# Loading half of the spectral filters behind the first bounce, and fewer feed-forward weights ahead of D

## The chip, the cores and the metric

The kernel runs on one core of a Trainium2 chip. The metric is device time in microseconds (us). Executions of one kernel mostly agree within 0.3%; the kernel before took 892.1 to 895.99 us in the runs that the prediction was made from.

Engines are called as in the profile: PE is TensorE (PEld its weight loads), DVE is VectorE, ACT is ScalarE, POOL is GpSimd, SP is SyncE, which here only issues DMAs. Every trace time is in us from the start of the span.

## The reference

Two layers, one behind the other. The first is a spectral filter over the sequence, the second a gated feed-forward block:

```
X = rfft(x, axis=1)              # x: 8 x 3008 x 256
y = irfft(X * (filt_r + 1j*filt_i), n=3008)
gate = maximum(y @ w_gate, 0)    # 256 x 1536
val  = y @ w_val                 # 256 x 1536
out  = (gate * val) @ w_out      # 1536 x 256
```

## The kernel before

The transform of length 3008 = 94 x 32 is done by matmuls in two stages. Stage A transforms over 94 and writes A to memory (`Abuf`); reading it back as `at` regroups it. I call this write and read the first bounce. Stage B, for six groups i: a forward matmul (`psX`), products with the filters (`tt` with the real part `Ftr`, `uu` with the imaginary part `Fti`), and an inverse matmul (`psD`) whose result D goes to memory (`Dbuf`). D comes back as `dC` (second bounce); stage C (`psY`) and the feed-forward matmuls V, G (`psV`, `psG`) and O (`psO`) follow. The first batch's B has nothing beside it; the later ones hide amid the feed-forward.

The filters lie in two copies along the partitions: GpSimd's DMA loads one, casting to bf16, and a copy (`place_filter`) makes the other. The code below is shortened; `...` stands where lines or arguments are left out.

```python
def load_filters():                      # eight loads, upper and lower groups together
    for src, dst in FILT:                # FILT = ((filt_r, Ftr), (filt_i, Fti))
        for a in range(2):
            r, k1, n = a * 64, 1 + 24 * a, NG - 2 * a
            nc.gpsimd.dma_start(dst[r:r + 31:2, 0:n, :], ...)       # rows that lie together
            yield
            nc.gpsimd.dma_start(dst[r + 1:r + 32:2, 0:n, :], ...)   # rows in reversed order

def place_filter(fi, a, half, copy):
    ...                                  # dst is Ftr or Fti, gs the half's groups, r = 64 * a
    copy(dst[r + 32:r + 64, gs, :], dst[r:r + 32, gs, :])

POOL_U = ((0, 1), (1, 0), (1, 1), (2, 0), (2, 1), (3, 1), (4, 0))   # products on GpSimd

def product(b, i, e, k, pool=False):
    ...
    if pool:
        nc.scalar.copy(xs, psX)                         # a copy for GpSimd to read
        nc.gpsimd.tensor_tensor(p, xs, filt, op=ALU.mult)
    else:
        nc.vector.tensor_tensor(p, psX, filt, op=ALU.mult)

def first_b(amid):
    ...
    for i in range(6):
        fwd(0, i)
        if i > 1:
            inv(0, i - 2, cuts=cuts)
        for e in range(2):
            product(0, i, e, 0)
            product(0, i, e, 1, pool=(i, e) in POOL_U)
        amid(i)                 # warming matmuls, then stage A of the next batch
    inv(0, 4, cuts=cuts); amid(6); inv(0, 5, cuts=cuts)
```

In the order of the program (cut):

```python
    next(filters)               # the first filter load, ahead of x
    ...                         # loads of x; the other seven wait for x's first half
    # stage A, load_at, then on DVE and ACT: all eight placements, place_nyq
    for i in range(14):
        warm(2)                 # idle matmuls that keep TensorE's clock up
    load_x(1, nc.sync, ((0, 0, 2 * q), (0, 2 * q, 4 * q), (1, 0, 4 * q)))   # the next batch
    ...
    hold_gpsimd(ats[0][0:32, NG - 1, 0:8])     # GpSimd waits for the first bounce
    load_vg(0, DFF // 2)                       # half of V's and G's weights
    first_b(amid)
    ...
    load_d(0, 0, 2)
    nc.gpsimd.dma_start(last, Dbuf[0][...])    # GpSimd waits for D's last write
    for c in range(2, 4):
        load_vg(c * DFF // 4, (c + 1) * DFF // 4)
```

## Time and profile before

| what (trace of the kernel before) | value |
|---|---|
| span of the profiled run | 892.0 us |
| first forward matmul of B (`psX`), end of the first bounce | 34.34 |
| third inverse (the one after the fifth forward): first 2 of its 16 matmuls | 43.02 |
| third inverse: the other 14, which wait for ScalarE's copies | 43.38 |
| last write of D issued | 51.03 |
| first stage C matmul (`psY`) | 57.35 |
| first O matmul (`psO`) | 72.59 |

TensorE is busy 98% of the span, and behind the first O matmul nothing else sets the pace. So whatever moves the first O matmul moves the end. The chain of waits shows which stage ends on what, the DMA use by queue shows who holds the 16 engines, and the timeline shows each engine's line. The prediction below shows those lines. One name there is off by one: what it calls "the one after the fourth forward" is the inverse behind the fifth, the third of six.

### The profile page before, as it was taken

To read this page: it belongs to the slowest core of one execution; us is meant where nothing else is said; L and a number is where in the kernel's file an instruction comes from. 1 tells how busy PE (TensorE), PEld (TensorE's weight loads), DVE (VectorE), ACT (ScalarE), POOL (GpSimd) and SP (SyncE) were. 2 spreads that over 40 slices of the span, in tenths; PEclk is the share of its full clock that TensorE was granted. 3 is DMA by queue.
4 is the path that set the end of the run, shared out by engine and by line. 5 is a ranking of instruction groups with operands and counts; after the bars stand their busy time and mean duration, and the time that the engine had idled before them with its cause. 6 is when DMAs were issued, how large, how long until landed. Compare 5 with 4: busy or idle time off the path is not lost.

```text
span 892.0 us, 19155 instructions
## 1 busy us (share of the span) xinstructions
PE 875.7 (98%) x7208; PEld 506.8 (57%) x7208; DVE 567.1 (64%) x871; ACT 504.2 (57%) x893; POOL 364.4 (41%) x361
## 2 busy tenths in 40 slices
PE   7899999999999999999999999999999999999997
PEld 2335655566556665566655565556655566666665
DVE  2736776577665766667766677657776577655553
ACT  4675555555655566556555556555655555555553
POOL 4350697038651476316671176802867000000001
PEclk9999999999999999999999999999999999999999
DMA  9997448534456336453376334662446512331111
GB/s 244 305 235 141 143 138 166 119 102 130 120 142 133 116 97 155 130 125 97 96 174 146 86 102 109 175 139 78 116 141 148 121 31 81 76 79 36 37 32 53
DMA packets 114099, 109.18 MB, mean 122 GB/s; under 512 B 20359, under 2 KB 98599, under 8 KB 113366
## 3 DMA queue, kind: packets, MB, share of 16 engines
q1 hardware_dynamic: 90294, 80.10, 34.7%
q0 software_dynamic: 22992, 26.41, 12.3%
q8 instruction: 57, 0.93, 0.5%
q10 hardware_dynamic: 720, 1.45, 0.4%
q14 instruction: 36, 0.29, 0.1%
HBM read 61.93 MB, written 49.81 MB: 125 GB/s over the span
## 4 chain that ended last, share of the span: by engine, by line
PE 93%; DMA 3%; ACT 1%; POOL 1%; issue 1%; DVE 0%; SPq 0%; ACTq 0%; POOLq 0%
PE psV L467 28%; PE psG L467 27%; PE psO L486 27%; PE psF L323 3%; PE psY L451 2%; PE psD L394 2%; PE psX L364 2%; PE psA L276 2%; DMA dC<-Dbuf 1%; DMA Abuf<-asb 1%; DMA at<-Abuf 1%; DMA XF<-in_x_dram 1%; ACT dsb L401 0%; DMA Dbuf<-dsb 0%; SPq L176 0%
## 5 line engine op out<-in xcount | busy, mean ns | idle before, releaser
L472 DVE SCALAR_TENSOR_TENSOR prod<-psG,vsb 128x512 bf16<-128x512 f32 x564 | 389.2, 690 | 263.6 <-ACT vsb L470 258.1
L470 ACT CAST vsb<-psV 128x512 bf16<-128x512 f32 x564 | 331.8, 589 | 263.0 <-PE psV L467 170.9
L467 PE MATMUL psV<-yT,WvT 128*128 128x512 bf16 x1128 | 336.6, 380 | 0.7 <-ACT asb L330 0.4
L486 PE MATMUL psO<-WoT,prod 128*128 128x256 bf16 x2256 | 336.5, 273 | 0.0
L467 PE MATMUL psG<-yT,WgT 128*128 128x512 bf16 x1128 | 335.4, 379 | 0.7 <-ACT dsb L401 0.3
L486 PEld LDWEIGHTS <-prod 128*128 128x128 bf16 x2256 | 220.2, 98 | 143.8
L467 PEld LDWEIGHTS <-WgT 128*128 128x128 bf16 x1128 | 109.9, 97 | 135.9 <-issue 2.5
L467 PEld LDWEIGHTS <-WvT 128*128 128x128 bf16 x1128 | 98.4, 98 | 41.9 <-issue 30.4
L258 POOL CAST scr<-prod 128x8 f32<-128x8 bf16 x24 | 4.5, 189 | 258.3 <-DVE prod L472 258.3
L509 POOL DMA_DIRECT2D out_dram<-osb x5 | 2.6, 536 | 195.9 <-ACT osb L499 195.9
L499 ACT COPY osb<-psO 128x512 f32<-128x512 f32 x92 | 53.9, 586 | 27.6 <-PE psO L486 26.1
L380 DVE TENSOR_TENSOR tt<-psX,Ftr 128x512 bf16<-128x512 f32 x96 | 65.1, 682 | 5.9 <-PE psX L364 5.9
L309 POOL TENSOR_TENSOR fold<-XP 128x1024 f32<-128x1024 f32 x24 | 56.5, 2355 | 20.5 <-PE psF L323 19.2
L380 DVE TENSOR_TENSOR uu<-psX,Fti 128x512 bf16<-128x512 f32 x89 | 60.6, 681 | 0.0
L401 ACT CAST dsb<-psD 128x512 bf16<-128x512 f32 x96 | 51.5, 589 | 12.1 <-PE psD L394 11.8
L296 POOL DMA_DIRECT2D XP<-in_x_dram x96 | 56.7, 596 | 3.2 <-PE psG L467 1.6
L310 POOL TENSOR_TENSOR XP<-XP 128x1024 f32<-128x1024 f32 x24 | 56.4, 2349 | 1.9
L330 ACT CAST asb<-psF 128x512 bf16<-128x512 f32 x48 | 25.8, 589 | 30.5 <-PE psF L323 30.5
L330 DVE CAST asb<-psF 128x512 bf16<-128x512 f32 x48 | 30.9, 686 | 18.6 <-PE psF L323 18.6
L456 ACT CAST yT<-psY 128x512 bf16<-128x512 f32 x47 | 27.5, 586 | 23.8 <-PE psY L451 23.6
L451 PE MATMUL psY<-M,dC 96*128 96x94 bf16 (+18 forms) x604 | 37.7, 199 | 1.4 <-DMA dC<-Dbuf 1.2
L458 DVE CAST yT<-psY 128x512 bf16<-128x512 f32 x47 | 32.0, 681 | 9.8 <-PE psY L451 9.8
(72 smaller groups left out, 493.5 us busy)
## 6 DMA issues: line engine op xcount, KB each, us to landing
at<-Abuf SPq DMA_DIRECT2D x32, 384.0 KB
dC<-Dbuf SPq DMA_DIRECT2D x64, 192.0 KB
XP<-in_x_dram POOLq DMA_DIRECT2D x48, 256.0 KB, 6.1
Dbuf<-dsb SPq DMA_DIRECT2D x23, 512.0 KB
XP<-in_x_dram POOLq DMA_DIRECT2D x96, 96.0 KB, 2.7
Abuf<-asb SPq DMA_DIRECT2D x96, 96.0 KB
out_dram<-osb SPq DMA_DIRECT2D x69, 94.0 KB
XF<-in_x_dram SPq DMA_DIRECT2D x15, 256.0 KB
```

Of the source, the lines that this page charges most:

```text
L296: nc.gpsimd.dma_start(xp[r:r + 24, 0:4:2, :], _ap(x, (b * N1 * N2 + o) * D, [[N2 * D, 24], [47 * N2 * D, 2], [1, 512]]))
L309: tt(t, xp[:, 0:2], xp[:, 2:4], op=ALU.add)
L310: tt(xp[:, 2:4], xp[:, 0:2], xp[:, 2:4], op=ALU.subtract)
L330: copy(asf[:, :, q, :], banks[q])
L380: nc.vector.tensor_tensor(p, psX, filt, op=ALU.mult)
L401: nc.scalar.copy(dsb[:, a, o:o + 2, :], psD[a])
L451: nc.tensor.matmul(psY[:, o:o + w], dCs[b, n2 // 8][:, n2 % 8, h * 128:(h + 1) * 128], M1[:, n1:n1 + w], start=True, stop=True)
L467: nc.tensor.matmul(pt[:, :W], w[:, h, ft * 128:(ft + 1) * 128], yt[:, h, :], start=(h == 0), stop=(h == 1))
L470: nc.scalar.copy(vsb, psV[:, :W])
L472: nc.vector.scalar_tensor_tensor(prod, in0=psG[:, :W], scalar=0.0, in1=vsb, op0=ALU.max, op1=ALU.mult)
L486: nc.tensor.matmul(psO[:, t % 2], prods[ft][:, t * 128:(t + 1) * 128], WoT[:, ft, :], start=(ft == 0), stop=(ft == NFT - 1))
L499: copy(osb[:, t0 % 2:t % 2 + 1], psO[:, t0 % 2:t % 2 + 1])
```

## The change

The filters' loads are cut into a lower and an upper half of the groups. The lower half stays where it was. The upper half is issued once the first bounce has landed, and placed on VectorE amid the first B, ahead of the products of group 3, the first that need it. GpSimd, now busy with issues, gives its products in groups 0 and 1 to VectorE and takes others. To leave the queue room, only a quarter of V's and G's weights goes ahead of D. Six warming matmuls go. The intent is to free the DMA engines for the first bounce.

```diff
-    def load_filters():
+    def load_filters(half):
+        g0 = H * half
         for src, dst in FILT:
             for a in range(2):
-                r, k1, n = a * 64, 1 + 24 * a, NG - 2 * a
+                r, k1, n = a * 64, 1 + 24 * a, H - 2 * a * half
 ... (both loads on groups g0 to g0 + n)
-    POOL_U = ((0, 1), (1, 0), (1, 1), (2, 0), (2, 1), (3, 1), (4, 0))
+    POOL_U = ((2, 0), (2, 1), (3, 0), (3, 1), (4, 0), (4, 1))
 ... (in first_b, behind fwd(0, i))
+            if i == 3:
+                for fi in range(2):
+                    for a in range(2):
+                        place_filter(fi, a, 1, nc.vector.tensor_copy)
+                place_nyq()
 ... (ahead of the first B: four placements of the lower half, all on VectorE)
-    for i in range(14):
+    for i in range(11):
         warm(2)
 ...
-    load_vg(0, DFF // 2)
+    for _ in load_filters(1):
+        pass
+    load_vg(0, DFF // 4)
 ...
-    for c in range(2, 4):
+    for c in range(1, 4):
         load_vg(c * DFF // 4, (c + 1) * DFF // 4)
```

More of the change, by code (lines that the diff above doesn't have):

```diff
@@ L213 @@
     nyq = []
-    def load_filters():
+    def load_filters(half):
+        g0 = H * half
         for src, dst in FILT:
             for a in range(2):
-                r, k1, n = a * 64, 1 + 24 * a, NG - 2 * a
-                nc.gpsimd.dma_start(dst[r:r + 31:2, 0:n, :],
-                                    _ap(src, k1 * D, [[N1 * D, 16], [1, n * D]]))
+                r, k1, n = a * 64, 1 + 24 * a, H - 2 * a * half
+                nc.gpsimd.dma_start(dst[r:r + 31:2, g0:g0 + n, :],
+                                    _ap(src, (k1 + g0) * D, [[N1 * D, 16], [1, n * D]]))
                 yield
-                nc.gpsimd.dma_start(dst[r + 1:r + 32:2, 0:n, :],
-                                    _ap(src, (N1 - k1) * D, [[N1 * D, 16], [-D, n], [1, D]]))
+                nc.gpsimd.dma_start(dst[r + 1:r + 32:2, g0:g0 + n, :],
+                                    _ap(src, (N1 - k1 - g0) * D, [[N1 * D, 16], [-D, n], [1, D]]))
     def load_own_filters():
@@ L525 @@
     nc.scalar.dma_start(tabs, nc.inline_tensor(tab_h, name="dft_tab").ap())
-    filters = load_filters()
+    filters = load_filters(0)
     next(filters)
@@ L550 @@
     warm(6)
-    place_filter(0, 1, 0, nc.scalar.copy)
     for i in range(3):
         make_back_u(i)
-    for a, half in ((0, 0), (0, 1), (1, 1)):
-        place_filter(0, a, half, nc.vector.tensor_copy)
     place_own()
-    for a, half, copy in ((1, 0, nc.scalar.copy), (0, 0, nc.vector.tensor_copy),
-                          (0, 1, nc.vector.tensor_copy), (1, 1, nc.vector.tensor_copy)):
-        place_filter(1, a, half, copy)
-    place_nyq()
-    for i in range(14):
+    for fi in range(2):
+        for a in range(2):
+            place_filter(fi, a, 0, nc.vector.tensor_copy)
+    for i in range(11):
         warm(2)
```

## The prediction

> **What bounds the kernel now.** I read the page first, then the chain that ended last up to the first block, then DMA use by queue in short windows, then the timeline there.
>
> ```profile
> PE 875.7 (98%) x7208; PEld 506.8 (57%) x7208; DVE 567.1 (64%) x871; ACT 504.2 (57%) x893; POOL 364.4 (41%) x361
> ```
>
> TensorE is busy 98% of 892 us. From about 60 us on, the chain is an unbroken run of V, G and O matmuls, so no later stage can give or take much. The change touches the first 75 us only, and the end moves by what moves the matmuls of the first block. The chain there (start, us, what):
>
> ```profile
> 12.82 10.53 PE psA L276 x24
> 23.37 0.59 ACT asb L279
> 23.98 5.43 DMA Abuf<-asb
> 29.47 4.78 DMA at<-Abuf
> 34.34 0.46 PE psX L364 x8
> ...
> 51.03 2.41 DMA Dbuf<-dsb
> 53.45 0.33 SPq L427
> 53.83 3.39 DMA dC<-Dbuf
> 57.35 0.62 PE psY L451 x12
> ```
>
> Stage A ends at 23.4 on TensorE; then comes the first bounce (A to memory and back), 10.4 us to the first psX at 34.34; then the first B, 16.7 us from there to the last write of D at 51.03; then the second bounce to 57.35. TensorE has 0.5 us of idle time in front of psY, so D's date sets the start of the first block. DMA by queue (packets, MB, share of 16 engines) in 18 to 22 us, then 22 to 26:
>
> ```profile
> q0 software_dynamic: 632, 0.61, 100.7%
> q1 hardware_dynamic: 56, 0.23, 15.0%
> ...
> q0 software_dynamic: 635, 0.47, 75.8%
> q1 hardware_dynamic: 180, 0.62, 41.1%
> ```
>
> q0 carries the filters, q1 the bounce. The filters hold the engines while A's writes want them: the packet records show A's second chunk written only at 21.1 to 23, though its last copy ended at 17.1, and the fourth, issued at 23.98, landing at 29.4. That wait is the change's target.
>
> **What the skill says.** The page DMA: Bandwidth & Descriptors, section Issuing engines are not separate DMA queues, says that queues of all issuers interleave on the same 16 engines; the same page, section SWDGE vs HWDGE vs iDMA, that a load which casts must be issued from GpSimd. The trace agrees: the filters (float to bf16) are on q0, and above q0 and q1 share one capacity. Its section Anatomy of one DMA gives some 2 us of fixed cost per GpSimd load. Here the issues of 34.84 had their first packet at 38.99, 4.1 us, and the first held filter load of 13.34 at 16.9, 3.5 us; with the engines free (54.58 to 56.85) it was 2.3 us. I use these.
>
> **Part 1: half of the filters leaves the bounce.** q0's shares in 14 to 30 us are 30.2, 100.7, 75.8 and 9.8% of four 4 us windows, 8.7 us of all engines. Half is 4.4 us. The backlog then ends near 23 us, just before A's last chunk is issued, which that issue at 23.98 bounds. Its landing should take about 3 us instead of 5.43. The return read, 3072 packets of 512 B, runs at 192 packets in 0.305 us once undisturbed, so 4.9 us; it began at 26.7 and had a straggling tail to 34.0. I expect it from 26.0 to 31.2, with a small tail: psX at about 31.9, so **2.4 us earlier** (1.5 to 3). VectorE's four placements (0.95 us each, row below) and 22 warming matmuls fit: they end near 30 and 31.
>
> **Part 2: the upper half is needed in the first B.** It is issued after the bounce, so its price is a new wait. The rows:
>
> ```profile
> L238 DVE COPY Ftr<-Ftr x3: 944/949/952, 25.8 to 27.6; 32x3072 bf16<-32x3072 bf16 x3
> L378 POOL TENSOR_TENSOR uu<-xs,Fti x7: 1143/1154/1156, 37.4 to 45.6; 128x512 bf16<-128x512 f32 x7
> ```
>
> GpSimd issues eight loads. In the timeline seven took 13.34 to 17.13, 0.54 us each, so 4.3 us. Starting 0.45 us after psX (31.9) they run 32.35 to 36.7, then V's and G's quarter (2 x 0.73) to 38.1. The first packet follows 3.5 to 4 us after the first issue: about 36.1. On q1 the next batch's x is flowing then. In the kernel before, its share was 95.9% in 35 to 40 us, against the weights' 5.3%, and the weights moved only afterwards:
>
> ```profile
> q1 hardware_dynamic: 228, 1.79, 95.9%
> q0 software_dynamic: 27, 0.04, 5.3%
> ...
> q0 software_dynamic: 436, 0.64, 72.9%
> q1 hardware_dynamic: 203, 0.55, 32.7%
> ```
>
> x starts behind the return read, at about 31.0, and takes some 8.5 us alone (it ran 32.5 to 42.7, with 1.5 us of q0 inside). At 36.1, 3.4 us of it are left; the upper filters are half of 8.7 plus half of the one contiguous load taken early, 4.8 us. Together 8.2 us, at the 1.05 to 1.15 by which the two queues' shares sum above one, is 7.5 us: 43.6. D's first write (256 packets of 2 KB at 84 ns, 1.3 us) falls in it. Straggling engines and the landing add about 1 us; I take the last filter landed at **44.5** (42 to 46).
>
> From there: the last placement 0.95, the two Nyquist rows 0.43, two products 0.7 (VectorE starts one per 0.61 us): 46.6, when the third inverse (the one after the fourth forward) can have its PSUM banks. That inverse started at 43.0 before, and D's last write was issued 8.0 us later, through two A chunks, the last forward and three inverses with TensorE in that order. The same 8.0 gives 54.6. The second way, four GpSimd products after the last placement (45.5 + 4 x 1.15 = 50.1), then inverse 4, an A item, inverse 5 and its two copies (3.5 us), gives 53.6, so it is not the later one. D's last write moves from 51.03 to about 54.6: **+3.5 us** (0 to +5), although the bounce ended 2.4 us sooner.
>
> **Part 3: three quarters of V and G behind D, not two.** Each quarter pair is 512 packets of 768 B at 78 ns: 2.5 us of the engines. In the timeline before (first line an issue, second and third the feed-forward matmuls):
>
> ```profile
> 56.72 0.75 POOL L246 DMA_DIRECT2D WgT<-in_moe_w_gate_dram  x1
> ...
> 65.45 0.60 PE L467 MATMUL psV<-yT,WvT 128*128 128x512 bf16 x2
> ...
> 65.88 0.59 PE L467 MATMUL psG<-yT,WgT 128*128 128x512 bf16 x2
> ```
>
> The third and fourth quarters land (issue plus time to landing) at V 60.4, G 62.9, V 64.5, G 67.8. In the changed kernel these four places in the queue hold the second and third quarters. The second is first read at 62.9 (V) and 63.3 (G): just in time. The third is read by the seventh feature tile, at 65.45 and 65.88 on this clock; G's part is there at 67.8: **a stall of about 1.9 us** in the first block. The fourth follows some 2 us later, about 70.8 against a need at 70.8 after the stall: 0 to 0.5. The output weights then land near 75, against 76 for the second group of O matmuls: no stall. In sum +2.0 us (0.5 to 2.5), counted from D.
>
> **The sum.** Start of the first block +3.5, stall inside it +2.0; the rest is bound by TensorE and unchanged; six fewer warming matmuls lie in a wait. 893.1 + 5.5 = 898.6. I shade this to **897.0** for the first rival.
>
> **The rivals.** (a) The upper filters come in time. If q0 gets an equal share against x and lands by 41, products 3 follow as before relative to psX, D is 1 to 2.4 us early, and the total is 891 to 893 with a stall or without. For it: the warm-up was cut by six matmuls, as if the shorter bounce was counted on, and GpSimd's products were moved to pairs 2 to 4, behind the issues. Against: the last filter issue ends only at 36.7, with 3.5 us to a first packet, and x is ahead. I give it a quarter. (b) The bounce does not shorten: q0's remainder still straggles and psX stays near 34. Then all of part 2 moves by about 2 us, to some 900. Against: the backlog before A's last chunk is 8.7 us of q0, and half is gone. (c) GpSimd becomes the bound: it is free only at 38.1, 6.2 us after psX, and the first inverse to read its products is the third. But 38.1 + 2.3 = 40.4 is still before the filters land, so the issue time is hidden. (d) The weights' stall vanishes because fewer bytes are in flight behind D: nothing in this change takes traffic out of 54 to 66 us, so I don't think so; it would give 895.
>
> **Range and chances.** All that can move is inside some 10 us of an 893 us kernel: at best 2.4 gained and no stall (890.7), at worst 5 lost and 2.5 of stall (900.6) plus run noise of 1 to 3 us (892.1 to 895.99). So 891.8 to 901.5, and 2% (17.9 us) is out of reach on either side.
>
> **What would show it.** Right: psX near 32; VectorE idle near 39 to 44 until filter DMAs; D's last write after 53; a gap of about 2 us at the seventh feature tile, ended by the weights' DMA. Wrong: last filter placed before 42, D's write before 51, or no gap in the first block. The step I trust least is the share that q0 gets against x.

## The result, and the profile after

The changed kernel took 905.65 us (median; 903.76 to 906.63 in 4 runs) against 893.61 for the kernel before in the same rounds. The ratio is 1.013, with a 95% interval of 1.0101 to 1.0158. The predicted direction was right; the time lies outside the range, and the loss of 12.0 us (span 904.0 against 892.0) is three times the 3.9 that was predicted.

On the page of the changed kernel TensorE is busy 879.1 us (97%) with 7202 matmuls, before 875.7 us (98%) with 7208: it does the same work, in a longer span.

The chain that ended last, of the changed kernel (start, us, what):

```profile
11.66 10.53 PE psA L277 x24
...
22.82 3.62 DMA Abuf<-asb
26.50 5.43 DMA at<-Abuf
...
36.03 8.12 DMA Fti<-in_filt_i_dram
...
61.02 2.41 DMA Dbuf<-dsb
...
68.14 12.88 DMA WgT<-in_moe_w_gate_dram
```

The first bounce did what was hoped: A's last chunk lands in 3.62 us instead of 5.43 (the read behind it takes 5.43 instead of 4.78), and the first forward starts at 32.03 instead of 34.34. Half of the 2.3 us is not the bounce, though: stage A's last 24 matmuls already started 1.16 us sooner (11.66 against 12.82). Then a filter load has entered the chain, with 8.1 us from its issue to its landing; D's last write has moved from 51.03 to 61.02; and a load of G's weights ends the waits of the first block.

| | before | after | difference |
|---|---|---|---|
| first forward of B | 34.34 | 32.03 | -2.31 |
| third inverse, the 14 matmuls that wait | 43.38 | 51.21 | +7.83 |
| last write of D issued | 51.03 | 61.02 | +9.99 |
| first O matmul | 72.59 | 84.79 | +12.20 |

So 10 us are lost in the first B and 2.2 in the first block behind it. What VectorE and GpSimd did in the first B is in the timeline of the changed kernel (start, us, engine, line, operation, count; in brackets the idle time before it and what ended it). First GpSimd, then VectorE:

```profile
38.71 0.73 POOL L247 DMA_DIRECT2D WvT<-in_moe_w_val_dram  x1 [2.13 <-DMA Ftr<-in_filt_r_dram]
42.72 0.90 POOL L247 DMA_DIRECT2D WgT<-in_moe_w_gate_dram  x1 [3.27 <-DMA Ftr<-in_filt_r_dram]
43.72 2.27 POOL L379 TENSOR_TENSOR uu<-xs,Fti 128x512 bf16<-128x512 f32 x2
```

```profile
42.52 4.29 DVE L239 COPY Ftr<-Ftr 32x3072 bf16<-32x3072 bf16 x2 [3.76 <-DMA Ftr<-in_filt_r_dram]
46.84 1.93 DVE L239 COPY Fti<-Fti 32x3072 bf16<-32x3072 bf16 x2
```

Three things are to be seen. VectorE idles 3.76 us until the first two filter loads have landed at 42.5. Then two copies take 4.29 us, while the next two, of the same size, take 1.93. And GpSimd, which the prediction had free at 38.1, issues its last weight load at 42.72: its ninth load waited for the landing of the first filter load and its tenth for the second. (The instruction records of the trace show why: GpSimd's loads use eight completion semaphores in turn, 99 to 106, and each waits for the load eight before it.) So its products, meant for 38 to 40, run from 43.72 to 46.0, in the middle of VectorE's copies. The copies one by one (duration in ns min/median/max, first and last start):

```profile
L239 DVE COPY Ftr<-Ftr x4: 950/952/3305, 26.5 to 43.5; 32x3072 bf16<-32x3072 bf16 x4
```

One copy took 3305 ns and the others 950. TensorE in the meantime waited 9.7 us in front of the third inverse. The wait ended on ScalarE's copy of a forward result for GpSimd (`xs`), and that copy had waited for VectorE's product:

```profile
51.21 0.42 PE L395 MATMUL psD<-tt,I2t 64*64 64x256 bf16 x2 [9.67 <-ACT xs L378]
49.92 1.24 ACT L378 COPY xs<-psX 128x512 f32<-128x512 f32 x2 [8.84 <-DVE tt L381]
```

TensorE's clock was lowered as well. Work by engine in one stretch (busy us and count of PE, PEld, DVE, ACT, POOL; then the granted clock, DMA share, GB/s):

```profile
46.00:56.00 10.00, 4.79 (x26) 1.71 (x29) 5.55 (x9) 4.33 (x9) 4.52 (x4) 0.51 0.04 6
```

For those ten us TensorE ran at half its clock, 0.51, and in 56 to 60 at full again (1.00). In the kernel before the clock is 1.00 in every ten-us stretch from 30 to 90.

In the first block, TensorE waits three times for weights:

```profile
77.23 0.60 PE L473 MATMUL psG<-yT,WgT 128*128 128x512 bf16 x2 [0.89 <-DMA WgT<-in_moe_w_gate_dram]
...
80.09 0.60 PE L473 MATMUL psV<-yT,WvT 128*128 128x512 bf16 x2 [0.30 <-DMA WvT<-in_moe_w_val_dram]
...
81.06 0.60 PE L473 MATMUL psG<-yT,WgT 128*128 128x512 bf16 x2 [0.36 <-DMA WgT<-in_moe_w_gate_dram]
```

The first is at the seventh feature tile, the first read of the third quarter, as predicted.

### The profile page after: what moved, and what is told of

The parts are those of the page before. It is cut to its first block, busy times and chain, and to the rows that moved or that the text cites. A ratio compares the mean times of both kernels' runs of the same rounds, so it can differ in the third digit from the quotient of the medians.

```text
span 904.0 us, 19153 instructions
## 1 busy us (share of the span) xinstructions
PE 879.1 (97%) x7202; PEld 508.2 (56%) x7202; DVE 572.1 (63%) x874; ACT 498.4 (55%) x890; POOL 368.9 (41%) x370
## 3 DMA queue, kind: packets, MB, share of 16 engines
q10 hardware_dynamic: 720, 1.45, 0.4%
## 4 chain that ended last, share of the span: by engine, by line
PE 90%; DMA 5%; SPq 1%; POOL 1%; DVE 1%; ACT 1%; issue 1%; ACTq 0%; POOLq 0%; DVEq 0%
PE psV L473 27%; PE psO L492 26%; PE psG L473 26%; PE psF L324 3%; PE psD L395 2%; PE psY L457 2%; PE psA L277 2%; PE psX L365 2%; DMA at<-Abuf 2%; DMA WgT<-in_moe_w_gate_dram 1%; DMA Fti<-in_filt_i_dram 1%; SPq L341 1%; DMA XF<-in_x_dram 0%; SPq L176 0%; DMA Abuf<-asb 0%
## 5 line engine op out<-in xcount | busy, mean ns | idle before, releaser
L297 POOL DMA_DIRECT2D XP<-in_x_dram x96 | 56.7, 596 | 2.8 <-PE psV L473 1.4
```

Of the source, the lines that this page charges most:

```text
L297: nc.gpsimd.dma_start(xp[r:r + 24, 0:4:2, :], _ap(x, (b * N1 * N2 + o) * D, [[N2 * D, 24], [47 * N2 * D, 2], [1, 512]]))
```

## The experiments

My theory after reading the traces had four causes: the weights behind D (2.2 us), the blocked copy (2.4), the lowered clock (1.8), and the filters' late landing with its copies. The first two runs part the weights from the filters, the next two take the blocked copy and the clock. The clocked times of such single repairs differ little from the changed kernel's, and some intervals overlap with its own; the steps are read from the traces, one profiled execution of each kernel. (The expectations count the runs by labels, in which there is no fifth.)

### The weights alone

```diff
 (kernel before)
-    load_vg(0, DFF // 2)
+    load_vg(0, DFF // 4)
-    for c in range(2, 4):
+    for c in range(1, 4):
```

> Only part 3: a quarter of V and G ahead of D, three behind; filters as before. Theory (weights arrive late): D's last write stays at 51.0 us in the trace (51.03 before), the first O matmul moves from 72.6 to about 74.8, with gaps of TensorE in the first block of 1.6 to 2.2 us in sum that end on the loads of V and G; time +2.0 to +2.4 us, ratio 1.0025. Rival (the 2.2 us between D and the first O matmul in the changed kernel come from the late D or the slow clock, not from the weights): first O matmul at 72.6, ratio 1.000.

In the trace the time from D's last write (50.62) to the first O matmul (74.08) is 23.46 us; it is 21.56 in the kernel before. The 1.9 us are one gap:

```profile
67.36 0.61 PE L467 MATMUL psG<-yT,WgT 128*128 128x512 bf16 x2 [1.73 <-DMA WgT<-in_moe_w_gate_dram]
```

The time was 894.98 us against 894.5, ratio 1.0004 (0.9987 to 1.0021). The interval holds 1, and the expected 1.0025 lies just outside it: in the clocked time this was a miss. The span of the profiled run is 893.9, 1.9 us above the profile of before, but other executions of the kernel before reach 893.9 too. So the wait and its size are shown in the trace; that it costs the whole run as much is not shown by this run's clock.

### The filters' part alone

```diff
 (changed kernel)
-    load_vg(0, DFF // 4)
+    load_vg(0, DFF // 2)
-    for c in range(1, 4):
+    for c in range(2, 4):
```

> Only the filters' part: the changed kernel with half of V and G ahead of D again. Theory: D's last write at about 61.0 as in the changed kernel (61.02), first O matmul 21.6 us later, at 82.6; 2.2 us faster than the changed kernel, ratio to before 1.011. Rival: the two weight loads behind the filters are twice as large and hold GpSimd longer, or contend with D's writes, so D comes later than 61.5; or the weights were not the stall, and the ratio stays 1.013.

D's last write was issued at 60.99, the first O matmul came at 82.53, 21.54 us later, as before. No wait for weights is left in the first block. Time 904.09, ratio 1.0109 (1.009 to 1.0129). This is as the theory had it: the weights cost 2.2 us behind D, and D's 10 us have nothing to do with them.

### GpSimd kept away from the copies

```diff
 (changed kernel)
-    POOL_U = ((2, 0), (2, 1), (3, 0), (3, 1), (4, 0), (4, 1))
+    POOL_U = ((3, 0), (3, 1), (4, 0), (4, 1))
```

> The changed kernel, but both products of the third pair (2,0) and (2,1) on VectorE, so GpSimd runs nothing from 43.7 to 46.0 while VectorE places the filters. Theory (VectorE's copy is blocked by GpSimd's product[...]): the second Ftr copy takes 0.95 us and not 3.3, the last placement ends near 46.5 and not 48.8, the third inverse and D's last write come 2.3 us sooner (58.7), time 2.3 us less than the changed kernel. Rival (that copy was slow for its data or for DMA traffic, and GpSimd has nothing to do with it): copy still above 3 us, D at 61.0 or up to 1.2 us later for two more products on VectorE.

VectorE's timeline of this run:

```profile
41.63 1.93 DVE L239 COPY Ftr<-Ftr 32x3072 bf16<-32x3072 bf16 x2 [1.82 <-DMA Ftr<-in_filt_r_dram]
43.60 1.93 DVE L239 COPY Fti<-Fti 32x3072 bf16<-32x3072 bf16 x2
```

All four copies take 0.95 us now, though GpSimd's loads wait for the same landings. D's last write is at 58.15, 2.9 us sooner than in the changed kernel; time 902.99, ratio 1.0096 (1.0074 to 1.0118). So GpSimd's product is what held the copy. (Of the 2.9 us, 2.4 are the blocked copy; the first filters also landed 0.9 us sooner here, and half of that was lost again behind the third inverse: from there to D it took 10.2 us, in the changed kernel 9.8.) The Trainium skill says why that can be, on the page SBUF — State Buffer, section Who interferes with whom: a VectorE copy in a mode that takes two ports and a GpSimd instruction need the same pair of ports, and the one that doesn't get it is blocked, not slowed (the later expectations call this the lock). The trace agrees, with 3305 ns against 950.

### TensorE kept busy in the wait

```diff
 (changed kernel, in first_b)
             fwd(0, i)
+            if i == 4:
+                warm(40)
```

> The changed kernel with 40 idle matmuls (8.6 us at full clock) between the fifth forward and the third inverse, where TensorE waits for the filters. Theory (the wait lets TensorE's clock drop to half from 46.0 to 56.2): granted clock 1.0 through 50 to 60 us, third inverse still at 51.2, D's last write 8.0 us after it as before and not 9.8, so at about 59.2; time 1.8 us less than the changed kernel. Rival (the 1.8 us are GpSimd's and ScalarE's work, not the clock): clock 1.0 but D's last write still 9.8 us after the third inverse, time unchanged.

Work by engine in 50 to 60 (columns as above), the changed kernel first, then this run:

```profile
50.00:60.00 10.00, 8.79 (x79) 3.55 (x79) 4.16 (x7) 8.04 (x16) 4.53 (x4) 0.71 0.23 75
```

```profile
50.00:60.00 10.00, 10.00 (x93) 4.09 (x91) 4.15 (x7) 9.19 (x18) 4.54 (x4) 1.00 0.35 118
```

The clock stays at 1.00 in 50 to 60; it is 0.71 there in the changed kernel. From the third inverse (51.70) to D's last write (59.57) it takes 7.9 us and not 9.8. D gains 1.45 us and not 1.8, because the idle matmuls held the third inverse 0.5 us back: the 40 of them took 10.1 us, not 8.6, for the clock was 0.83 in 40 to 50. Time 903.31, ratio 1.0097 (1.0082 to 1.0112). The Trainium skill's page TensorE: Matmul & The Clock Gate, section Why this matters for your kernels, says to leave no idle gap above about 3 us between bursts of matmuls, or the clock falls to half. The wait of 9.7 us in the changed kernel agrees.

### All three repairs

```diff
 (changed kernel)
     POOL_U = ((3, 0), (3, 1), (4, 0), (4, 1)); warm(18) at i == 4;
     load_vg(0, DFF // 2) ahead of D and two quarters behind it
```

> The changed kernel with all three repairs at once: third pair's products on VectorE, 18 idle matmuls in the wait for the filters, half of V and G ahead of D. Theory (the three causes add, and what is left is the filters' late placement): D's last write near 56.7 (61.02 less 2.9 less 1.4), first O matmul 21.6 us behind it at 78.3, time 5.7 us above the kernel before, ratio 1.0063. Rival (the causes overlap, one hides behind another): ratio 1.008 or more; or nothing else is left: ratio 1.002 or less.

D's last write came at 55.72 (expected 56.7), the first O matmul at 77.34; time 899.83, ratio 1.0058 (1.0036 to 1.008). The causes add up, with 1.0 us more gained than their sum, and 4.7 us of D's delay remain. They belong to the filters' landing on the one hand, and to their placing and the products that VectorE took over on the other; the next three runs tell the landing from the rest.

### The same, with x out of the filters' way

```diff
 (repaired kernel; also warm(10) in place of warm(18))
-    load_x(1, nc.sync, ((0, 0, 2 * q), (0, 2 * q, 4 * q), (1, 0, 4 * q)))
+    load_x(1, nc.sync, ((0, 0, 2 * q), (0, 2 * q, 4 * q)))
 ... (in first_b, behind amid(i), so SP issues it behind D's first write)
+            if i == 3:
+                load_x(1, nc.sync, ((1, 0, 4 * NX2 * D // 4),))
```

> The repaired kernel with the last three loads of the next x (512 KB each, not read before D) issued behind D's first write, so they no longer run beside the filters. Theory (the filters land late because x holds the engines): the last filter lands near 41.5 and not 43.5 to 44.2, VectorE's wait in front of the placements (1.8 us in the third run) vanishes, D up to 1.8 us earlier than the repaired kernel, ratio about 1.0045. Rival (the lateness is GpSimd's issue and descriptor time, not x): landing and D unchanged, ratio 1.006.

Time from issue to landing of the upper half of Fti (min/median/max): the repaired kernel first, then this run. (In the changed kernel the median is 8.5.)

```profile
DMA to landing us min/median/max: 7.7/7.9/7.9
```

```profile
DMA to landing us min/median/max: 3.8/3.8/4.0
```

The filters land in half the time, and the copies start as soon as VectorE is done with its products, with no wait before them:

```profile
40.31 1.93 DVE L239 COPY Ftr<-Ftr 32x3072 bf16<-32x3072 bf16 x2
```

So x's loads did make the landing late. But D only moved from 55.72 to 54.36, and that is still 3.3 us behind the kernel before, although now nothing waits for a filter and the forward starts 2.0 us sooner than there (32.34). Ratio 1.0019 (1.0004 to 1.0033). My prediction had said that filters in time would make D early. That fell here.

### The copies late, the loads early

```diff
 (kernel before: its loads, its warm loop of 14, and half of V and G ahead)
     upper half placed in first_b at i == 3 and POOL_U, as in the changed kernel;
     lower half placed ahead of the first B, all four copies on VectorE
```

> The kernel before, all its loads where they were, but the upper half placed between products 3 as in the changed kernel and GpSimd's products those of the changed kernel. Theory (the placing itself costs: 3.9 us of VectorE copies and 0.4 of Nyquist rows stand in its line between products 2 and 3, with the filters long landed): psX at 34 as before, placements from about 41.0 to 45.3, third inverse near 47.3 and not 43.0, D near 55, ratio 1.0045. Rival (only the landing matters, placing hides in VectorE's idle time): D at 51 to 52, ratio 1.000.

All filters had landed long before. The first forward was at 34.54, yet D's last write came only at 58.68, 7.7 us later than before; time 901.04, ratio 1.0074 (1.0057 to 1.0091). That was worse than either theory: I had left out that GpSimd's products meet the copies here too, and that TensorE waits 5.3 us:

```profile
41.09 2.78 DVE L238 COPY Ftr<-Ftr 32x3072 bf16<-32x3072 bf16 x2
43.90 2.76 DVE L238 COPY Fti<-Fti 32x3072 bf16<-32x3072 bf16 x2
```

Four copies take 5.5 us and not 3.9 (two of them 1.8 us each, and the two GpSimd products beside them 1.9 us each and not 1.15), and from the third inverse (49.09) to D it takes 9.6 us, with a granted clock of 0.84 in 50 to 60.

### The copies late, without block and with the clock up

```diff
 (kernel of the run just told)
-    POOL_U = ((2, 0), (2, 1), (3, 0), (3, 1), (4, 0), (4, 1))
+    POOL_U = ((3, 0), (3, 1), (4, 0), (4, 1))
 ... (in first_b)
+            if i == 4:
+                warm(22)
```

> The eighth run's kernel (all loads early, upper half placed late) with the two repairs for lock and clock: third pair's products on VectorE, 22 idle matmuls in the wait. It isolates what the place of the copies costs when nothing is late, nothing blocks and the clock is full. Theory (VectorE has no slack of four copies in the first B): four copies in 3.9 us from about 42.2 to 46.1, third inverse near 48.5 against 43.0 before, D near 56.3, so +5.3 us, ratio 1.006. Rival (what made the eighth run slow was only the lock and the clock): D at 52 or sooner, ratio 1.001 or less.

Within 0.6 us of what was expected: third inverse at 49.00, D at 56.87, ratio 1.0062 (1.0045 to 1.0078). Nothing is late, nothing blocks, the clock is full from 40 to 60 (1.00), and D still comes 5.8 us later than before. VectorE's timeline shows its line without a gap:

```profile
41.49 0.68 DVE L380 TENSOR_TENSOR uu<-psX,Fti 128x512 bf16<-128x512 f32 x1
42.20 1.92 DVE L238 COPY Ftr<-Ftr 32x3072 bf16<-32x3072 bf16 x2
44.15 1.92 DVE L238 COPY Fti<-Fti 32x3072 bf16<-32x3072 bf16 x2
...
46.48 2.48 DVE L380 TENSOR_TENSOR tt<-psX,Ftr 128x512 bf16<-128x512 f32 x4
```

In the kernel before, the products of group 3 start at 40.49, behind a wait:

```profile
40.49 0.69 DVE L380 TENSOR_TENSOR tt<-psX,Ftr 128x512 bf16<-128x512 f32 x1 [1.44 <-PE psX L364]
```

They start 6.0 us later now. The 6.0 us are: five products that GpSimd did before and VectorE does now, at 0.61 us each (3.05), plus the four copies and two Nyquist rows (4.3), less the 1.44 us that VectorE sat idle ahead of group 3 before (5.9 in sum). This split is arithmetic on the trace: no run moves the copies alone and leaves GpSimd its five products, so what each of the two would cost by itself is not shown.

### Only the smaller first load, twice

Stage A's earlier start in the changed kernel (1.16 us) has its own cause. I suspected the filter load that is issued ahead of x: in the program x's seventh load uses the completion semaphore of the first constant matrix again, and so must wait for that matrix. Halving that filter load alone on the kernel before:

```diff
 (kernel before, in load_filters; m is H for the first load only, n otherwise)
-                nc.gpsimd.dma_start(dst[r:r + 31:2, 0:n, :], ...)
+                nc.gpsimd.dma_start(dst[r:r + 31:2, 0:m, :], ...)
                 yield
+                if first:
+                    nc.gpsimd.dma_start(dst[r:r + 31:2, m:n, :], ...)   # waits with the rest
```

> The kernel before with one thing of the change alone: the filter load issued ahead of x is cut to its lower half, the other half waits with the rest. Theory (that load delays the landing of the first matrix, and the seventh x load waits for it, which is why the changed kernel's stage A ran 1.15 us sooner): third x block's matmuls at 11.7 to 12.0 and not 12.4 to 12.8, psX 0.5 to 1 us sooner, ratio 0.999. Rival (the sooner start is chance between runs): 12.4 to 12.8 and ratio 1.000.

Stage A's third block started at 11.97, psX at 33.66, D's last write at 50.58; time 893.56 against 895.07, ratio 0.9987 with an interval of 0.9972 to 1.0002. I ran it again with five rounds:

> The ninth run's kernel again, with more rounds: ratio there 0.9987 with an interval that contains 1. Theory (the smaller first filter load starts stage A's third block some 0.6 us sooner and D 0.45 us sooner): ratio 0.9985 to 0.9997, D's last write near 50.6. Rival (chance): ratio 1.000, D at 51.0.

This time the third block started at 12.13 but took 12.2 us instead of 10.5 (granted clock 0.94 over the first 30 us), psX was at 34.30, D at 50.99, and the time 893.17 against 894.5: ratio 0.9991 (0.9977 to 1.0005). Both are below one and neither is clear of it. The sooner start is there in both; whether a gain reaches the end stays open. This is the only kernel with a ratio below one.

The reason I gave is not what the traces show. The matrix had landed by 3.5 us both before and after the change, and x's seventh load was issued only at 6.93 and 5.98. What differs is the issue of x's fourth load on SP: it took 1.65 us in the kernel before and 0.59 in the changed one. Over all twelve traces it took 1.58 to 1.95 us in the four with the whole filter load ahead of x (third block from 12.39 to 12.82), and 0.59 to 0.91 us in the eight with half of it (11.66 to 12.13). What holds that issue is not shown.

## Why the prediction was right or wrong, point by point

**What bounds the kernel: right.** All of the difference arises before the first O matmul (+12.20), and the span grew by 12.0.

**Part 1, the bounce: right in size, half right in cause.** Predicted: psX at 31.9; measured 32.03. But 1.16 of the 2.31 us came from the sooner stage A, which the prediction didn't see, and 1.15 from the bounce, for which it had 2.4. That the sum fits so well is in part luck. Rival (b), no shorter bounce at all, is out.

**Part 2, the landing: right.** The last filter was predicted to land at 44.5 and landed at 44.15. The step on the share that q0 gets against x, which I trusted least, held, and the run with x moved away shows that it was x. (Two slips there, on which nothing rests: by the packet records the weights' first packet came at 38.76, not 38.99; and the page's some 2 us of fixed cost run to a load's completion, while the 4.1, 3.5 and 2.3 us set beside them run to its first packet.)

**Part 2, from the landing to D: wrong, and this is the step that failed.** It said: "From there: the last placement 0.95, the two Nyquist rows 0.43, two products 0.7 [...]: 46.6" and "The same 8.0 gives 54.6". It charged one copy behind the last landing, as if the other three would have been done by then, and it took GpSimd's late products for hidden (rival c: "so the issue time is hidden"). The trace has, from the landing at 44.15:

| term of the sum | predicted | measured |
|---|---|---|
| last landing to the end of the last placement | 0.95 | 4.6 (44.15 to 48.78) |
| Nyquist rows | 0.43 | 0.4 |
| then to the third inverse | 0.7 | 2.0 (49.19 to 51.21) |
| third inverse to D's last write | 8.0 | 9.8 |

The first row is 2.36 us of blocking (3305 less 950 ns) and, beyond it, copies in a row, because the first filters landed at 42.5, hardly sooner than the last; four copies from there end at 46.4 even unblocked. The third row has a slip of its own: two products at one per 0.61 us take 1.3, not 0.7. And it left out that ScalarE's copy of a forward result for GpSimd waits for VectorE's product on the same result, and the third inverse needs the PSUM banks that those copies free: the wait in front of it, 9.67 us, ended on that copy. The fourth row is the clock: the runs in which TensorE was kept busy take 7.8 to 7.9 us for it, the other runs with the late copies 9.6 to 10.3. (The 8.0 were counted from the third inverse's first two matmuls, at 43.02; from the 14 that wait, as in the measured column, it is 7.65 in the kernel before.)

All the signs that were named for "right" came: psX near 32, VectorE idle until the filters (38.8 to 42.5), D's last write after 53, the gap at the seventh tile. "D's write after 53" set no upper end, so the signs could not tell a D at 54.6 from one at 61.02.

**A rival that I judged wrongly.** Rival (a) made the landing the deciding thing: in time, and D is 1 to 2.4 us early. With the filters in time and all repairs D is 3.3 us late. The four copies in VectorE's line, together with the products taken from GpSimd so that it can issue loads, cost 5.8 us on their own, more than the bounce gives back. The runs put D's delay together in steps, each a difference of two runs' last writes of D. Each is one trace of each kernel, and even the kernels with the same loads and x in the way differ among themselves (VectorE's first late copy starts from 41.6 to 42.5 in five traces), so a step is good to about 1 us:

| step | D's last write | difference |
|---|---|---|
| kernel before | 51.03 | |
| copies late, clean (loads early) | 56.87 | +5.84 |
| upper half loaded behind the bounce, x out of the way | 54.36 | -2.51 |
| x beside the filters | 55.72 | +1.36 |
| GpSimd against the copies, and the clock | 61.02 | +5.30 |

The last row also holds the change of the weights, which the second run shows to be without effect on D (60.99).

**Part 3, the weights: right.** Predicted 2.0 us at the seventh feature tile; measured 2.2 from D to the first O matmul (23.77 less 21.56), in gaps at the seventh and tenth tiles. Undone, it vanishes (21.54), so rival (d) is out.

**The shading: wrong.** The sum was 898.6 and I shaded it to 897.0 for rival (a), which the runs show to be false. The range allowed D to be at most 5 us later; it was 10.

## What to carry to other kernels

Moving a load behind a busy stretch of DMA is not free if a copy comes with it: ask first whether the engine that must place the data has idle time in its own line at the new place. Here VectorE had 1.44 us of slack ahead of the group, and the placing wanted 4.3. Then look at what a delayed engine will run into: GpSimd's late products blocked VectorE's copies, and TensorE's long wait halved its clock, and these two turned a loss of some 5 us in D into one of 10. When a part needs more than eight loads in flight on one queue, look in the program for what the ninth waits for.

## What the Trainium skill lacked or had wrong

- DMA: Bandwidth & Descriptors says nothing on what it costs when a program has fewer completion semaphores than loads in flight. Here the loads used eight in turn, and GpSimd's ninth and tenth loads waited 2.13 and 3.27 us for the landing of the first two, and held the engine's products from some 38 to 43.7 us.
- SBUF — State Buffer, Who interferes with whom, says that the loser is blocked for the whole instruction of the other. In the changed kernel the copy, recorded from 43.5, was blocked through two GpSimd products in a row (43.72 to 46.0; 3305 ns against 950), though its recorded start is the earlier one; in the run with early loads two copies took some 1.8 us each and two products 1.9, so there it looks as if the engines took turns. By the page the one that issues first holds the ports; that doesn't tell which of the two to expect.
- TensorE: Matmul & The Clock Gate gives about 3 us of idle as the limit. In the changed kernel an idle gap of 2.29 us, ahead of psX, was followed by half the clock for some 3.4 us (0.83 in 30 to 40), while gaps of 2.14 us (kernel before) and 2.28 us (the run with idle matmuls) were followed by full clock (1.00). So a gap below the limit can lower the clock too, in some runs. No run here shows that this one cost time: VectorE's products went on without a gap.
